# Threshold attention and its expert layer in half batches: order of query tiles, sums, values, units, weight loads

## The chip, the core and the metric

One core of one Trainium2 chip runs the whole kernel. The metric is device time in microseconds from the first to the last instruction with what lies around them; three runs of the kernel before gave a median of 540.56 us (539.83 to 540.8). The engines are TensorE (PE; its weight loads are shown as PEld), VectorE (DVE), ScalarE (ACT), GpSimd (POOL) and SyncE (SP, which here only issues DMAs).

## The reference

```python
batch, n_heads, seq, head_dim = (8, 8, 576, 64)          # q, k, v
scores = scale * np.matmul(q, k.transpose(0, 1, 3, 2))
thresh = np.max(scores, axis=-1, keepdims=True) - tau
scores = np.where(scores >= thresh, scores, -1000000000.0)
scores = scores - np.max(scores, axis=-1, keepdims=True)
attn = np.exp(scores)
attn = attn / (np.sum(attn, axis=-1, keepdims=True) + 1e-09)
attn_out = np.matmul(attn, v)
x = attn_out.transpose(0, 2, 1, 3).reshape(B * S, H * D)  # 4608 x 512
h = x @ w_in                                              # 512 x 2048
g = np.maximum(0.01 * h, h)
out = g @ w_out                                           # 2048 x 512
```

Attention in which only scores within tau = 0.02 of a row's largest count, for 8 batches of 8 heads, and then a two-layer net ("the expert layer") over all 4608 tokens.

## The kernel before

Two heads make a pair, 32 pairs in all, four to a batch. Two pairs make a group c, so that a batch has two groups. A group's 2 x 576 queries are cut into nine query tiles of 128: t = 0 to 3 of the first pair, 4 to 7 of the second, and t = 8, which holds the last 64 queries of both. One such tile is a step; there are 16 x 9 = 144 steps, and nine more turns of the loop in which only what is left over is done. The order of all work is written out by hand in the main loop: engines run their queues in that order.

A step's own work. `s_mm` (L158) makes the scores of the tile, for both heads, in twelve pairs of half-height matmuls over hi and lo parts of q and k (24 small ones where t = 8), into PSUM tiles "s", one of two banks for each head. `s_max` (L181) reduces them on DVE, once per head: sn is the negated scaled score, nmx its least. POOL adds tau (L186, nth). Then either ACT takes the exponent (L191, e), and a step later `s_mask` (L214) masks it on DVE and sums it into den; or, where `direct` is set, ACT alone does both for the second head (L197 far, L201 W). At the end of `s_mask` a transposing DMA on SP's queue (L220) puts the tile's weights W into wT, from which `values` reads.

Work that is spread over the steps:

- `prep` transposes q (i = 0) or k and the two tails (i = 1) of a pair on PE (L129), into the PSUM pair of banks "A", of which there is one; ACT makes hi (L138), DVE makes lo at the end of the step (L139).
- The sums of a group: `sums_0` at t = 0 of the next group on POOL (L228), `sums_1` at t = 1 (reciprocal on DVE, L234, and its fp16 part on POOL, L235), `sums_2` after the step's second reduction (the remainder on DVE, L240), `sums_3` (a matmul that turns the columns into a row, L246, and ACT's copy, L249), and `sums_4` at t = 2 and 4, which spreads the row over partitions (L263, ACT L268, rc). All these use "A".
- `values` at t = 3 and 5 (L279), 20 matmuls each for one pair's 576 queries into "A"; DVE multiplies by rc at the end of that step (L289, xT), and POOL copies the last 64 tokens to xE (L293).
- The expert layer is a list of units. An h unit (`h_unit`, L301, L305) is four matmuls of 512 columns over the four pairs and a leaky rectifier on ACT into gM; sixteen make gM for 512 tokens of a batch. An out unit (`out_mm`, L316) is four of the sixteen matmuls of one output tile of 128 tokens; the fourth part is copied by ACT (L327) and every second tile stored by SP. Tails of two batches share four h units of 16 matmuls with 128 columns, and four out units. Units use the PSUM tiles "u", two banks.

`push_main` puts a batch's 32 units on the list at t = 6 of the group after the batch (the first at step 24), when all four pairs of the batch have their values. `share` weighs how many units each step takes; a step does half of them after its first reduction and half after the second.

Loads: q and k of pair 2c+3 and 2c+4 are issued by SP, one DMA a step (`load_qk`, L81, L86); v by POOL, at steps 1 to 5 for the first batch and at t = 4 to 8 of every even group after that (`load_v`, L96); the 16 pieces of w_in and 16 of w_out by POOL, one each at steps 1 to 32 (`load_w`, L105, L109).

Of the kernel before, what the change touches and what calls it, by code (L numbers as in the profile page):

```python
# [16 lines left out]
def kernel(  # L17
# [17 lines left out]
    NT = 9  # L35
# [14 lines left out]
    sel = sb.tile([128, 18, 64], FP16, name="sel")  # L50
    w_in16 = sb.tile([128, 4, d_ff], FP16, name="win16")
    w_out16 = sb.tile([128, NJ, d_model], FP16, name="wout16")
    gM = sb.tile([128, NJ, 512], FP16, name="gM")
# [7 lines left out]
    nat, qk, wTs, xTs = {}, {}, {}, {}  # L61
# [60 lines left out]
    def prep(p, i, tag="A", bufs=1):  # L122
# [13 lines left out]
        hi = sb.tile([128, N], FP16, tag=f"hi{i}", bufs=3, name=f"hi{i}")  # L136
        lo = sb.tile([128, N], FP16, tag=f"lo{i}", bufs=3, name=f"lo{i}")
# [7 lines left out]
    def s_mm(c, t):  # L145
# [3 lines left out]
        if t < 8:  # L149
            srcs = [(2 * c + t // 4, 0, ds(t % 4 * 128, 128), ds(0, 128))]  # L150
        else:
            srcs = [(2 * c + e, 1, ds(576, 64), ds(64 * e, 64)) for e in range(2)]
# [10 lines left out]
        sc[(c, t)] = out  # L163
# [3 lines left out]
    def s_max(c, t, h, direct):  # L167


        s_ = sc[(c, t)][h]  # L170
        if t == 0 and h == 0:
            dens[c] = sb.tile([128, 18], FP32, tag="den", bufs=2, name="den")
        if h == 0:
            sn = sb.tile([128, 2, 576], FP32, tag="sn", bufs=3, name="sn")
            nmx = sb.tile([128, 2], FP32, tag="nmx", bufs=4, name="nmx")
            nth = sb.tile([128, 2], FP32, tag="nth", bufs=4, name="nth")
            e = sb.tile([128, 2, 576], FP16, tag="e", bufs=3, name="e")
            live[(c, t)] = (sn, nmx, nth, e, Ws[wn[0] % len(Ws)], set())
            wn[0] += 1
        sn, nmx, nth, e, w, masked = live[(c, t)]  # L180
# [13 lines left out]
        else:  # L194
# [8 lines left out]
                accum_out=dens[c][:, 2 * t + h:2 * t + h + 1],  # L203
            )

    def s_mask(c, t):
        sn, nmx, nth, e, w, masked = live.pop((c, t))
        sc.pop((c, t))
        if t == 0:

            wTs[c] = sb.tile([128, 9, 1152], FP16, tag="wT", bufs=2, name="wT")
        for h in range(2):
            if h not in masked:
# [3 lines left out]
                    accum_out=dens[c][:, 2 * t + h:2 * t + h + 1],  # L217
                )
        q0 = 512 if t == 8 else t * 128 + (t // 4) * 128
        nc.sync.dma_start_transpose(out=wTs[c][:, :, ds(q0, 128)], in_=w[:, :])  # L220
# [3 lines left out]
    def sums_0(c):  # L224

        d1 = sb.tile([128, 18], FP32, tag="d1", bufs=1, name="d1")
        rr = sb.tile([128, 18], FP32, tag="rr", bufs=1, name="rr")
        nc.gpsimd.tensor_scalar(out=d1[:, :], in0=dens.pop(c)[:, :], scalar1=1.0, scalar2=1e-9,  # L228
                                op0=OP.mult, op1=OP.add)
        inv[c] = (d1, rr)  # L230

    def sums_1(c):
        d1, rr = inv[c]
        nc.vector.reciprocal(out=rr[:, :], in_=d1[:, :])  # L234
        nc.gpsimd.tensor_scalar(out=r2[:, 0, 0:18], in0=rr[:, :], scalar1=1.0 / RS, scalar2=0.0,  # L235
                                op0=OP.mult, op1=OP.add)

    def sums_2(c):
        d1, rr = inv[c]
        nc.vector.scalar_tensor_tensor(out=r2[:, 1, 0:18], in0=rr[:, :], scalar=1.0 / RS, in1=r2[:, 0, 0:18],  # L240
                                       op0=OP.mult, op1=OP.subtract)

    def sums_3(c):

        t = pair_of_banks().rearrange("p a b -> p (a b)")
# [4 lines left out]
        rows[c] = row  # L250

    def sums_4(c, e):

        row = rows[c]
        t = pair_of_banks().rearrange("p a b -> p (a b)")

        if e == 0:
            parts = [(2 * s, s * 128, 0, 128) for s in range(4)] + [(16, 512, 0, 64)]
        else:
            parts = [(16, 0, 64, 64)] + [(8 + 2 * s, 64 + s * 128, 0, 128) for s in range(3)]  # L260
            parts += [(14, 448, 0, 64), (14, 512, 64, 64)]
# [5 lines left out]
        rc = sb.tile([128, 576], FP32, tag="rc", bufs=2, name="rc")  # L267
        nc.scalar.activation(out=rc[:, :], in_=t[:, 0:576], func=AF.Copy, bias=0.0, scale=1.0)  # L268
        rcs[e] = rc

    def values(c, e):

        b, g = divmod(2 * c + e, NG)
        wT, vb = wTs[c], Vs[b % 2]
        t = pair_of_banks()
        for half in range(2):
            for kb in range(5):
                for h in range(2):
                    nc.tensor.matmul(  # L279
                        out=t[ds(h * 64, 64), half, 0:288], lhsT=vb[:, g, h, kb, :],  # L280
                        rhs=wT[:, 4 * h + kb, ds(e * 576 + half * 288, 288)],
                        start=(kb == 0), stop=(kb == 4), skip_group_check=True,
                    )
        rc = rcs.pop(e)
        x = sb.tile([128, 576], FP16, tag=f"xT{g}", bufs=2, name=f"xT{g}")
        xTs[(b, g)] = x

        def mul():
            nc.vector.tensor_tensor(  # L289
                out=x.rearrange("p (a b) -> p a b", a=2), in0=t[:, :, 0:288],  # L290
                in1=rc.rearrange("p (a b) -> p a b", a=2), op=OP.mult,
            )
            nc.gpsimd.tensor_copy(out=xE[g][:, b, :], in_=x[:, 0:64] if e else x[:, 512:576])  # L293
# [41 lines left out]
    def push_main(b):  # L335

        xs = [xTs[(b, g)][:, ds(g % 2 * 64, 512)] for g in range(NG)]
# [179 lines left out]
```

## Time and profile before

| | us |
|---|---|
| median of three runs | 540.56 |
| span of the profiled execution | 538.3 |
| PE busy | 497.8 (92%) |
| DVE busy | 421.7 (78%) |
| ACT busy | 433.8 (81%) |
| POOL busy | 188.1 (35%) |
| first reduction of step 0 starts | 10.13 |
| first reduction of step 24 starts | 83.03 |
| first reduction of step 126 starts | 426.53 |
| scores of step 143 start | 482.19 |

The span runs from the first to the last instruction of the one profiled execution. Busy time of PE counts the pipelined length of a matmul (380 ns for 512 columns that follow each other every 216 ns or so), so a busy PE need not be at its peak; spacing is read from the starts. In tables of windows, each engine has its busy time and its count of instructions, then come the granted TensorE clock (1.00 is full speed), the mean busy share of the 16 DMA engines and GB/s. In lists of waits, the three numbers are total us, times, and the longest; a weight load (PEld) and the matmul behind it wait for the same thing.

### The profile page before, as it was taken

How to read it: one execution, taken by the hardware profiler on the slowest of the kernel's cores; microseconds unless marked ns; L12 is line 12 of the kernel's file. 1: busy time of each engine (PE TensorE's matmuls, PEld its weight loads, DVE VectorE, ACT ScalarE, POOL GpSimd, SP SyncE). 2: the span in 40 equal slices, each digit the busy share in tenths (PEclk: the TensorE clock that was granted, in tenths of full speed). 3: DMA queues.
4: the chain of work that ended last, by engine and by line, in shares of the span. 5: the costliest groups of instructions: out<-in, count | busy, mean ns of one | idle time of the engine just before them, and what ended most of it. 6: DMA issues, size and time to landing. Idle time of an engine off the chain costs nothing.

```text
span 538.3 us, 12333 instructions
## 1 busy us (share of the span) xinstructions
PE 497.8 (92%) x4384; PEld 272.8 (51%) x4384; DVE 421.7 (78%) x1106; ACT 433.8 (81%) x765; POOL 188.1 (35%) x430
## 2 busy tenths in 40 slices
PE   5678679899999999999999999999999999999996
PEld 3345454454545565454545566455545566445444
DVE  4897989988899878987899878987899878982000
ACT  3887879899878989889888989889888989884622
POOL 0754556443433334222432234323432234331000
PEclk9676969999999999999999999999999999999999
DMA  6999999998998699778999799777998699654001
GB/s 151 150 202 161 175 182 214 200 180 173 172 165 136 139 169 196 140 137 153 183 155 143 132 182 185 142 135 159 183 155 136 132 187 135 111 89 106 39 40 58
DMA packets 266814, 80.50 MB, mean 150 GB/s; under 512 B 251905, under 2 KB 264193, under 8 KB 266753
## 3 DMA queue, kind: packets, MB, share of 16 engines
q1 hardware_dynamic: 249136, 70.68, 72.3%
q0 software_dynamic: 17536, 8.92, 14.2%
q8 instruction: 34, 0.56, 0.4%
q14 instruction: 28, 0.22, 0.1%
q10 hardware_dynamic: 80, 0.13, 0.1%
HBM read 36.70 MB, written 9.44 MB: 86 GB/s over the span
## 4 chain that ended last, share of the span: by engine, by line
PE 43%; ACT 25%; DVE 16%; issue 8%; DMA 4%; POOL 3%; SPq 0%; DVEq 0%; ACTq 0%; POOLq 0%
PE u L316 13%; DVE sn L181 11%; PE u L301 10%; PE s L158 10%; PE A L279 8%; ACT e L191 7%; ACT far L197 5%; ACT W L201 5%; DVE W L214 3%; ACT gM L305 3%; ACT hi L138 3%; POOL nth L186 3%; DMA nat<-in_q_dram 2%; DVE lo L139 1%; ACT rc L268 1%
## 5 line engine op out<-in xcount | busy, mean ns | idle before, releaser
L181 DVE TENSOR_SCALAR_CACHE_REDUCE sn<-s 128x576 f32<-128x576 f32 x288 | 206.5, 750 | 49.3 <-PE s L158 49.1
L186 POOL TENSOR_SCALAR nth<-nmx 128x1 f32<-128x1 f32 x288 | 127.4, 442 | 251.7 <-DVE sn L181 229.5
L191 ACT ACTIVATE e<-sn,nmx 128x576 f16<-128x576 f32 x196 | 150.5, 769 | 32.4 <-DVE sn L181 32.2
L214 DVE SCALAR_TENSOR_TENSOR W<-sn,nth,e 128x576 f16<-128x576 f32 x196 | 155.6, 814 | 0.0
L301 PE MATMUL u<-xT,win 128*128 128x512 f16 x512 | 128.9, 380 | 2.5 <-ACT gM L305 2.5
L316 PE MATMUL u<-wout,gM 128*128 128x512 f16 x512 | 126.2, 380 | 0.0
L158 PEld LDWEIGHTS <-hi 64*128 64x128 f16 (+1 forms) x1280 | 65.1, 99 | 70.2 <-issue 54.9
L158 PE MATMUL s<-hi,hi 64*128 64x288 f16 x512 | 86.2, 300 | 10.3 <-DVE sn L181 8.8
L158 PE MATMUL s<-lo,hi 64*128 64x288 f16 (+1 forms) x640 | 92.2, 294 | 0.0
L158 PE MATMUL s<-hi,lo 64*128 64x288 f16 (+1 forms) x640 | 92.1, 294 | 0.0
L301 PEld LDWEIGHTS <-win 128*128 128x128 f16 x768 | 58.7, 98 | 56.5 <-issue 20.1
L305 ACT ACTIVATE gM<-u 128x512 f16<-128x512 f32 x128 | 74.6, 588 | 11.7 <-PE u L301 11.7
L197 ACT ACTIVATE far<-sn,nth 128x576 f32<-128x576 f32 x92 | 71.0, 771 | 13.8 <-POOL nth L186 11.6
L201 ACT ACTIVATE W<-far,ntau 128x576 f16<-128x576 f32 x92 | 71.3, 775 | 3.0
L316 PEld LDWEIGHTS <-gM 128*128 128x128 f16 x512 | 44.7, 98 | 51.3 <-issue 12.3
L139 DVE SCALAR_TENSOR_TENSOR lo<-A,hi 128x512 f16<-128x512 f32 (+1 forms) x63 | 47.6, 756 | 14.2 <-ACT hi L138 13.7
L129 PE MATMUL A<-I,nat 128*128 128x128 f32 x283 | 44.6, 288 | 9.9 <-DVE lo L139 4.7
L279 PE MATMUL A<-wT,V 128*64 128x288 f16 x640 | 47.5, 297 | 1.5 <-ACT rc L268 1.1
L129 PEld LDWEIGHTS A<-I,nat 128*128 128x128 f32 x283 | 35.2, 147 | 25.2 <-DVE lo L139 10.0
L138 ACT ACTIVATE hi<-A 128x512 f16<-128x512 f32 (+1 forms) x63 | 40.0, 636 | 7.6 <-PE A L129 7.6
L279 PEld LDWEIGHTS <-V 128*64 128x64 f16 x640 | 36.6, 113 | 11.9 <-issue 8.4
L158 PEld LDWEIGHTS <-lo 64*128 64x128 f16 (+1 forms) x640 | 32.1, 99 | 12.6 <-issue 8.9
(44 smaller groups left out, 292.1 us busy)
## 6 DMA issues: line engine op xcount, KB each, us to landing
nat<-in_q_dram SPq DMA_DIRECT2D x32, 256.0 KB, 3.8
nat<-in_k_dram SPq DMA_DIRECT2D x32, 256.0 KB, 3.9
out_dram<-osb SPq DMA_DIRECT2D x16, 512.0 KB, 3.0
wT<-W SPq DMA_TRANSPOSE x144, 3.9
V<-in_v_dram POOLq DMA_DIRECT2D x8, 256.0 KB, 6.1
win<-in_moe_w_in_dram POOLq DMA_DIRECT2D x16, 128.0 KB, 5.2
V<-in_v_dram POOLq DMA_DIRECT2D x16, 128.0 KB, 4.7
wout<-in_moe_w_out_dram POOLq DMA_DIRECT2D x16, 128.0 KB, 4.3
```

The source lines that it names most:

```text
L129: nc.tensor.matmul(out=pt[0:128, ds(c * 128, 128)], lhsT=t[0:128, 4 * i + c, :, :].rearrange("p h d -> p (h d)"), rhs=I32[:, :], is_transp ...
L158: nc.tensor.matmul(out=out[h][po, half, 0:288], lhsT=qk[p][i][a][r, cols], rhs=qk[p][1][b][r, ds(half * 288, 288)], start=(ti == 0), stop= ...
L181: nc.vector.tensor_scalar(out=sn[:, h, :].rearrange("p (a b) -> p a b", a=2), in0=s_[:, :, 0:288], scalar1=-BS, scalar2=None, op0=OP.mult, ...
L186: nc.gpsimd.tensor_scalar(out=nth[:, h:h + 1], in0=nmx[:, h:h + 1], scalar1=1.0, scalar2=tau_f, op0=OP.mult, op1=OP.add,)
L191: nc.scalar.activation(out=e[:, h, :], in_=sn[:, h, :], func=AF.Exp, bias=nmx[:, h:h + 1], scale=-1.0,)
L197: nc.scalar.activation(out=far[:, :], in_=sn[:, h, :], func=AF.Prelu, bias=nth[:, h:h + 1], scale=-1.0, alpha=BIG,)
L201: nc.scalar.activation(out=w[:, ds(h * 576, 576)], in_=far[:, :], func=AF.Exp, bias=ntau[:, 0:1], scale=1.0, accum_out=dens[c][:, 2 * t + ...
L214: nc.vector.scalar_tensor_tensor(out=w[:, ds(h * 576, 576)], in0=sn[:, h, :], scalar=nth[:, h:h + 1], in1=e[:, h, :], op0=OP.is_le, op1=OP ...
L279: nc.tensor.matmul(out=t[ds(h * 64, 64), half, 0:288], lhsT=vb[:, g, h, kb, :], rhs=wT[:, 4 * h + kb, ds(e * 576 + half * 288, 288)], star ...
L301: nc.tensor.matmul(out=t[:, ts(j, N)], lhsT=w_in16[:, gi, ts(j0 + j, 128)], rhs=xs[gi], start=(gi == 0), stop=(gi == NG - 1), skip_group_c ...
L305: nc.scalar.activation(out=g_out, in_=t[:, 0:nj * N].rearrange("p (j n) -> p j n", j=nj), func=AF.Prelu, bias=0.0, scale=1.0, alpha=0.01)
L316: nc.tensor.matmul(out=t[:, :], lhsT=g_in(j), rhs=w_out16[:, j, :], start=(j == 0), stop=(j == NJ - 1), skip_group_check=True,)
```

## The change

A batch is worked through in 18 steps instead of two groups of nine. Its steps go through four sets of tiles G = (b, gi): gi = 0 and 1 are the first two query tiles of the pairs 0, 1 and of the pairs 2, 3 (four steps each), gi = 2 and 3 are the tail tile and the other two query tiles of the same pairs (five steps each). So after eight steps the first half of the queries of all four pairs are done.

- Sums, the row and its spreading are done for each G: four chains in a batch, at t = 5, 9, 14 and 1 of the next batch, on 8 or 10 columns. `sums_3` and `sums_4` take their PSUM tile from "u" and no longer from "A".
- `values` runs for each G in two parts of ten matmuls, 256 or 320 columns wide, in two steps that follow each other; one multiplication on DVE ends both.
- The units come by half batch u: eight h units of eight matmuls with 256 columns, and eight out units. `push_main(b, 0)` comes at t = 12 of the batch itself (the first at step 12), `push_main(b, 1)` at t = 6 of the next. gM is two tiles of half the size. The number of units and of their rectifiers is the same.
- Units a step come from a rate that looks at every push to come; `share` and the choice of direct steps are new.
- `prep` runs at steps 0 to 5 for the pairs 1 to 3 of the first batch; hi and lo have four buffers and wT three, for three and two.
- v of the first batch is issued ahead of step 0, later ones at t = 12 to 16; the pieces of w_in at steps 0 to 10 and of w_out at 11 to 18, up to two a step; pair 3 wholly at step 0, the pairs of the next batch at t = 2 to 17.

```diff
+    def place(st):
+        b, i = divmod(st, NS)
+        gi = 0 if i < 4 else 1 if i < 8 else 2 if i < 13 else 3
+        pos = i - (0, 4, 8, 13)[gi]
+        e = pos // 2 if gi < 2 else (pos - 1) // 2
+        tile_c = pos % 2 if gi < 2 else 2 + (pos - 1) % 2
+        tail = gi > 1 and pos == 0
+        return (b, gi), pos, 4 * b + gi % 2 * 2, e, tile_c, tail
...
-    def sums_3(c):
-        t = pair_of_banks().rearrange("p a b -> p (a b)")
+    def sums_3(G):
+        t = bank()
...
-    def sums_4(c, e):
-        row = rows[c]
-        t = pair_of_banks().rearrange("p a b -> p (a b)")
+    def sums_4(G, e):
+        row = rows[G]
+        t = bank()
...
-        for half in range(2):
-            for kb in range(5):
-                for h in range(2):
-                    nc.tensor.matmul(
-                        out=t[ds(h * 64, 64), half, 0:288], lhsT=vb[:, g, h, kb, :],
-                        rhs=wT[:, 4 * h + kb, ds(e * 576 + half * 288, 288)],
+        for kb in range(5):
+            for h in range(2):
+                nc.tensor.matmul(
+                    out=t[ds(h * 64, 64), e, 0:N], lhsT=vb[:, g, h, kb, :],
+                    rhs=wT[:, 4 * h + kb, ds(e * N, N)],
...
-        for j in range(NJ):
-            units.append((1, lambda j=j: h_unit(512, xs, gM[:, j:j + 1, :], j, 1)))
+        for j in range(0, NJ, 2):
+            units.append((1, lambda j=j: h_unit(256, xs, gM[:, j:j + 2, :], j, 2)))
...
+        for i in range(5):
+            load_v(0, i)
+        share = (22, 22, 22, 22, 13, 13, 27, 13, 13, 27, 13, 13, 22, 22, 22, 13, 13, 22)
+        for b in range(B):
+            pushes[NS * b + 12] = 16
+            pushes[NS * b + 24] = 16 + 4 * (b % 2 == 1 or b > 1) + 4 * (b == B - 1)
...
+                    st = 2 * j + i - 2 if b == 0 else o + ((-6, -5), (-4, -1), (0, 1), (2, 3))[j][i]
+                    if st >= 0:
+                        preps[st] = (4 * b + j, i)
...
+                st = o + (4, 8, 13, 18)[gi]
+                close[st] = G
+                chain[st + 1] = G
+                spread[st + 2] = (G, 0)
+                if gi > 1:
+                    spread[st + 3] = (G, 1)
+                v0 = o + (7, 10, 15, 22)[gi]
+                (early if gi < 2 else late)[v0] = (G, 0)
+                early[v0 + 1] = (G, 1)
...
+        for i in range(32):
+            w_at.setdefault(i * 11 // 16 if i < 16 else 11 + (i - 16) // 2, []).append(i)
...
-                    direct = tau_f <= 16.0 and (
-                        t not in (3, 7) if c < 3 else t in (3, 5) or not any(u[0] for u in units[:n]))
+                direct = tau_f <= 16.0 and (
+                    t not in (3, 7) if st < 12 else t in (5, 8, 11, 16) or not any(u[0] for u in units[:n]))
```

In a step the order is now: scores; `prep` (in the first batch); the `early` values; the first reduction; `sums_1`; the first half of the units; `prep`; the `late` values; `sums_4`; the second reduction; `sums_2`, all but one of the second half of the units, `sums_3` and that unit where a chain falls; else the second half of the units; `s_mask` of the step before; lo and the multiplication; `sums_0`; loads.

More of the change, by code (lines that the diff above doesn't have):

```diff
@@ L222, with cols_of @@
     inv, rows, rcs = {}, {}, {}
[L224 to L228, printed above, removed]
[L229 to L235 removed]
+    def cols_of(G):
+        return 8 if G[1] < 2 else 10
@@ new lines @@
+            if st in chain:
+                sums_1(chain[st])
+            work(n - n // 2)
+            if pi is not None:
+                prep(*pi)
+            if st in late:
+                values(*late[st])
+            if st in spread:
+                sums_4(*spread[st])
+            if not last:
+                s_max(st, 1, direct)
+            if st in chain:
+                sums_2(chain[st])
+                work(n // 2 - 1)
+                sums_3(chain[st])
+                work(1 if n > 1 else 0)
+            else:
+                work(n // 2)
```

302 lines of the change are left out of this document (166 added, 136 removed).

## The prediction

> **What bounds the kernel now.** I read the table of windows first, cut at steps: a step is one query tile, 144 in all, and it starts where the first reduction of L181 starts. The cuts are step 0 (10.13), 12, 24, 36 (123.03), 54, 72, 90, 108, 126 (426.53), and 482.19, where the scores of step 143 start.
>
> ```profile
> core 0: us, PE busy (x) PEld busy (x) DVE busy (x) ACT busy (x) POOL busy (x), PEclk, DMA share, GB/s
> 10.13:46.03 35.90, 25.88 (x192) 14.98 (x191) 31.27 (x83) 29.21 (x50) 20.38 (x42) 0.71 1.13 176
> 46.03:83.03 37.00, 27.52 (x276) 17.56 (x276) 33.69 (x89) 28.95 (x50) 18.87 (x41) 0.82 1.14 176
> 83.03:123.03 40.00, 37.65 (x337) 19.90 (x336) 35.74 (x95) 36.35 (x66) 19.94 (x43) 1.00 1.25 194
> 183.20:243.70 60.50, 59.55 (x573) 33.78 (x573) 52.61 (x138) 53.76 (x97) 21.32 (x49) 1.00 0.91 160
> 482.19:538.30 56.11, 51.42 (x341) 26.07 (x340) 6.42 (x17) 22.40 (x39) 2.29 (x7) 0.99 0.20 59
> ```
>
> Three stages. Steps 0 to 23 (72.9 us) have no expert units: DVE leads (31.3 of 35.9), PE's clock is partly halved. From step 24 on units fill PE; a batch of 18 steps takes 60.2 to 61.2 us, mean 60.7 over steps 36 to 125, with PE busy 98%. After step 143, 56 us remain in which PE works nearly alone. Now PE's stream and DVE's, for prices (the second column is the length, so spacing is read from the starts):
>
> ```profile
> 245.02 1.03 PE L316 MATMUL u<-wout,gM 128*128 128x512 f16 x4
> 245.98 0.30 PE L158 MATMUL s<-hi,hi 64*128 64x288 f16 x2
> 246.12 0.28 PE L158 MATMUL s<-hi,lo 64*128 64x288 f16 x2
> ...
> 246.61 0.29 PE L158 MATMUL s<-lo,hi 64*128 64x288 f16 x2
> 246.82 1.90 PE L316 MATMUL u<-wout,gM 128*128 128x512 f16 x8
> 249.33 0.23 PE L246 MATMUL A<-I,r 128*128 128x128 f16 x1 [0.61 <-DVE r L240]
> ```
> ```profile
> 183.98 0.71 PE L129 MATMUL A<-I,nat 128*128 128x128 f32 x5
> 184.52 1.03 PE L316 MATMUL u<-wout,gM 128*128 128x512 f16 x4
> ```
> ```profile
> 317.95 1.06 PE L301 MATMUL u<-xE,win 128*128 128x128 f16 x16
> ```
> ```profile
> 481.15 0.75 DVE L181 TENSOR_SCALAR_CACHE_REDUCE sn<-s 128x576 f32<-128x576 f32 x1
> 481.83 0.81 DVE L214 SCALAR_TENSOR_TENSOR W<-sn,nth,e 128x576 f16<-128x576 f32 x1
> 482.57 0.82 DVE L214 SCALAR_TENSOR_TENSOR W<-sn,nth,e 128x576 f16<-128x576 f32 x1
> 483.31 0.75 DVE L181 TENSOR_SCALAR_CACHE_REDUCE sn<-s 128x576 f32<-128x576 f32 x1
> ```
>
> A 512-wide matmul is spaced (1.03-0.38)/3 = 0.217, so a unit of four is 0.866; a 128-wide one (1.06-0.22)/15 = 0.056; a transpose 0.54/5 = 0.108; a pair of score matmuls 0.122. A change between tiled shapes (64*128 or 128*64) and the full array costs 0.09 more (the last pair of scores is followed after 0.21, not 0.12). DVE: reduction 0.68, mask 0.74; lo 0.61 or 0.74, xT 0.67 in the same way. Waits of PE and its weight loads in the 303.5 us of steps 36 to 125:
>
> ```profile
> PE u L301 <- ACT gM L305: 2.0, 8, 0.3
> PEld L246 <- DVE r L240: 8.9, 10, 1.4
> ```
>
> So the one real wait of steady state is the matmul of the sums, 0.89 us each, two a batch. Check by addition, PE of one batch: 18 scores x (6 x 0.122 + 2 x 0.093) = 16.6; 34 units x 0.866 + 2 tail units of 16 x 0.056 = 31.2; 36 transposes 3.9; 4 values x (10 x 0.122 + 0.095) = 5.2; sums 1.1: 58.0. With waits of 2 x 0.89 = 1.8 and 0.9 of small ones it is the measured 60.7. PE sets the steady state.
>
> **The change, part by part.**
> *Units by half batch.* The same 288 units, 128 of them now 8 matmuls of 256 columns. No row has that width; the bounds are 8 x 0.056 (too little) and 8 x 0.217; interpolating 0.056 at 128 and 0.217 at 512 gives 0.109, a unit 0.87. Cost 0.1 a batch. ACT's Prelu stays 128x512.
> *Values by half.* Eight blocks of ten matmuls for four of twenty, the same columns. The six that run right after the scores add one change of shape (0.095), the two in mid-step two (0.19): 0.95 for 0.38, +0.57 a batch.
> *Sums by half batch.* Four chains a batch for two. One more matmul of 0.06 each is little; the wait is not. From the first score matmul of the step to the sums' matmul I find 2.85 to 3.57 us (three cases; 245.98 to 249.33 is 3.35): scores, reduction, reciprocal, reduction, remainder on DVE. In front of it PE now has: t=5, scores 0.83, half a value block 0.75, one unit: 2.45, DVE on time: wait 0.4. t=9, two units: 2.56, but steps 7 and 8 carry 2.8 and 3.5 us of DVE against 2.54 of PE in every other batch, so DVE comes late: 1.2. t=14 and t=1, one unit and a transpose block: 2.3, waits 0.9 and 1.0. Sum 3.5 a batch against 1.8. Behind the waiting matmul stand units and the next scores, so DVE and ACT wait too. Bounds: 4 x 0 and 4 x 1.4 (the longest seen).
> *Sums in the unit banks.* Ten tiles a batch move from A to u, two buffers. A unit after such a tile reuses the bank of the unit just before it, and waits for its Prelu. Bounds: none, or ten waits of 0.3; about three fall where PE has nothing between: 0.8.
> *Push.* Units of t=12 may need an xT that DVE finishes just then: 0.2.
> Steady batch: 58.0+0.1+0.6+0.1 = 58.8 of PE, +3.5+0.8+0.9+0.2 = 64.2 (bounds of the waits: 61 to 67). Masks and direct rows stay alike (196 to 198 masks).
> *Steps 0 to 23.* Transposes of three pairs of a batch crowd into steps 0 to 5, two sum chains fall before step 12. DVE's sum by step (ACT's where larger) is 33.8 for steps 0 to 11 and 38.7 for 12 to 23, against 32.0 and 33.7 before; measured before were 35.9 and 37.0, 7.2 above the sums, since PE at half clock and the sums lengthen the loop of scores and reductions. With more PE work the half clock shrinks, so I add 3.1 and 1.8: 36.9 and 40.5, +4.5. In return 16 units are done by step 36; steps 24 to 35: 40.5 for 40.0.
> *Loads.* Five V issues (0.68 each on POOL) go ahead of step 0, hidden in POOL's first idle 9.7 us; their bytes share the DMA engines with pairs 1 and 2, which lands them some us later, still ahead of their transposes at steps 0 to 3: 0.4 (0 to 2). Pair 3's four loads go into SP's queue at step 0, ahead of the first transposing DMA, which isn't ready yet. Weights come one or two a step (0.57 each on POOL, which is busy 57% there): nothing waits for POOL but the small nth. No cost taken, up to 6 if DMA chokes.
> *The end.* At step 143's scores before, 53 units were left; after, 3+12+24 = 39: 33.8, with scores 0.83, values 1.6, sums 0.5, one xT 0.3 and the last copy and store 4.6 (533.7 to 538.3): 41.8 for 56.1, -14.3.
>
> Sum against the span of 538.3: +0.4 +4.5 +0.5; steps 36 to 53 (two units fewer) 62.5 for 60.2, +2.3; steps 54 to 125 4 x 64.2 = 256.8 for 243.3, +13.5; steps 126 to 143's scores 58.1 for 55.7, +2.4; end -14.3. Together +9.3: span 547.6. The median of the runs is 2.3 above the profiled span: **549.9**, say 549.5.
>
> Two rules. The rows show the 128-wide matmuls at 0.056 although each has a weight load of 0.098. The Trainium skill (TensorE: Matmul & The Clock Gate, Back-to-back issue gap) gives about 81 ns for a load and matmul pair at N=128 in a real kernel, 25 ns above this row; on the added 1024 narrow matmuls that would be 25.6 us and 575. The windows show a granted clock of 0.71 and 0.82 in steps 0 to 23, so (1-0.71) x 2 x 35.9 + (1-0.82) x 2 x 37.0 = 34 us at half. The same page (Terms) puts the penalty at throttled time x (1 - K/N), 17 us; by it, ending the half clock would give back 17, not the 2.3 of my sum, and 535.
>
> **Rivals.**
> 1. The waits don't grow: the sums' chain is covered as now, PE's loss stays 2.7 a batch. Batch 61.5; changes +0.4, +2.5, 0, -0.4, +2.7, 0, -14.3: 529.2, with 2.3 **531.5**, faster. For it: DVE has 13% idle in steady state, and half batches let lateness average out. Against: the wait is met at all ten chains looked at. It decides below about 0.6 us of added waits a batch (2.7 in my sum). 22%.
> 2. Loads choke: DMA share is 1.1 to 1.25 already, and by step 18 some 3 MB more (14 weights, V, a pair) must pass at about 200 GB/s seen; with transposing DMAs (3.9 us) landing after 6 or more, values before step 12 and first units wait: +8, **557**. Against: landings of 4 to 7 us there show little queueing. 10%.
> 3. In between, gains and waits cancel: waits 2.1 below my sum a batch: **540.5**. 6%.
> 4. Clock: PE is what the half clock holds up; 34 us at half are 17 us of cycles, and all come back: 549.5 + 2.3 - 17 = **535**. Against: DVE is busy 33.7 of 37.0 us there. 3%.
> 5. Weight loads show between narrow matmuls: 512 more at up to 0.098 exposed, half of it taken: 25 us, **575**. Against: the 0.056 row. 2%.
> The forecast has 57%, its own range 542 to 557.
>
> A difference under 0.2% (1.1 us) can't be told from none. Faster: rivals 1 and 4, less their spill into none: 0.23. Same: 0.06. Slower: the rest, 0.71. For eight in ten the range reaches down to rival 1 and up past rival 2: 531 to 559.
>
> **What would show it.** The sums' matmul with four waits a batch of 0.4 to 1.2 each; 18 steps taking 63 to 65 us from step 54 on with PE's idle on that line and on unit banks; 256-wide matmuls spaced 0.109; steps 0 to 23 in 76 to 79 us; 42 us from the last scores to the end. A batch at 61.5, or an added 256-wide spacing over 0.12, makes it wrong.

## The result, and the profile after

| | before | after |
|---|---|---|
| median of the runs taken side by side, us | 540.43 (four) | 581.93 (four: 576.51 to 582.95) |
| ratio, 95% interval | | 1.0755 [1.0708, 1.0802] |
| span of the profiled execution, us | 538.3 | 579.3 |
| PE / DVE / ACT / POOL busy, us | 497.8 / 421.7 / 433.8 / 188.1 | 511.0 / 425.5 / 442.3 / 192.1 |

The change makes the kernel slower by 7.5%, 41.5 us. PE is busy 13.2 us longer; the rest of the 41 us in the span is time in which PE does nothing. Medians here and below are of all runs; the ratios leave out one slow run, the 576.31 us of the kernel with the sums behind all units.

The table of windows of the changed kernel, cut as before at steps 0, 12, 24, 36 and 54, then steps 72 to 89, and last the stretch from the scores of step 143 on (engines' busy time and count, granted clock, DMA share, GB/s):

```profile
12.70:51.89 39.19, 28.37 (x236) 16.43 (x236) 32.36 (x87) 29.61 (x52) 19.32 (x45) 0.78 1.14 175
51.89:102.17 50.28, 39.67 (x344) 23.77 (x343) 36.95 (x99) 34.30 (x63) 22.57 (x53) 0.90 1.11 162
102.17:145.25 43.08, 39.21 (x406) 25.24 (x404) 33.62 (x93) 36.41 (x67) 15.80 (x37) 1.00 1.00 158
145.25:210.20 64.95, 60.72 (x622) 38.13 (x621) 53.63 (x146) 53.50 (x97) 22.11 (x53) 1.00 0.83 150
276.00:342.80 66.80, 62.01 (x638) 39.71 (x636) 53.91 (x146) 54.53 (x99) 22.12 (x53) 1.00 0.81 143
534.94:579.30 44.36, 37.59 (x305) 24.76 (x303) 6.48 (x17) 18.66 (x34) 2.54 (x9) 0.99 0.29 67
```

DVE's work grew by 1 to 3 us in the first two windows and in a batch (32.36 for 31.27, 36.95 for 33.69, 53.91 for 52.66 in steps 72 to 89), these windows by 3 to 13: steps 12 to 23 went from 37.0 to 50.3 us. Put in one table, with the prediction's terms (the last row starts at step 143's scores, the one above ends there):

| stage | before | predicted | after | after - predicted |
|---|---|---|---|---|
| to step 0's first reduction | 10.1 | 10.5 | 12.7 | +2.2 |
| steps 0 to 23 | 72.9 | 77.4 | 89.5 (39.2 and 50.3) | +12.1 |
| steps 24 to 35 | 40.0 | 40.5 | 43.1 | +2.6 |
| steps 36 to 53 | 60.2 | 62.5 | 64.9 | +2.4 |
| steps 54 to 125, four batches | 243.3 | 256.8 | 265.3 (65.8, 66.8, 65.8, 67.0) | +8.5 |
| 126 to the scores of 143 | 55.7 | 58.1 | 59.4 | +1.3 |
| from there to the end | 56.1 | 41.8 | 44.4 | +2.6 |
| span | 538.3 | 547.6 | 579.3 | +31.7 |

So 22 us of the loss against before, and 8.5 of the miss, lie in the four steady batches; 14.3 of the miss lie ahead of step 24.

PE's waits in the steady batches, steps 54 to 125 (total us, times, longest), changed kernel:

```profile
PE u L334 <- ACT gM L338: 5.6, 20, 0.5
PE u L265 <- ACT gM L338: 4.7, 4, 1.3
PE u L265 <- DVE r L259: 2.7, 8, 0.8
PE u L349 <- ACT osb L360: 2.0, 4, 0.5
PE u L349 <- ACT row L268: 1.4, 2, 0.7
PE u L334 <- ACT row L268: 1.4, 2, 0.7
PE u L334 <- ACT gE L338: 0.9, 2, 0.5
```

Before, the same list held 4.5 us in all for those steps:

```profile
PE A L246 <- DVE r L240: 2.5, 6, 0.6
PE u L301 <- ACT gM L305: 1.4, 6, 0.3
PE A L279 <- ACT rc L268: 0.6, 4, 0.2
```

Now it holds 18.7: 2.7 for the remainder, and 16.0 for something that ACT has yet to copy out of a bank of "u": a unit's rectifier (gM, gE), an output (osb) or the row. (A list counts from the modelled end of the matmul ahead, so a wait measured from start to start is 0.1 to 0.2 longer.) L265 is the matmul of the sums, L334 an h unit, L349 an out unit. Two things are to be seen. The sums' matmul itself waits for a rectifier, once a batch, at t = 9, for 1.0 or 1.3 us, because the bank it is given still holds a unit. And units wait for the row, or for the unit just before them.

The timeline of step 78 of the changed kernel shows both (start, length, engine, line, operation, then in brackets the idle time before and its releaser; rows of weight loads, DVE, POOL and SP are left out, and so are rows of PE and ACT where dots stand):

```profile
296.39 0.23 PE L265 MATMUL u<-I,r 128*128 128x128 f16 x1
296.46 1.03 PE L349 MATMUL u<-wout,gM 128*128 128x512 f16 x4
297.15 0.78 ACT L209 ACTIVATE far<-sn,nth 128x576 f32<-128x576 f32 x1 [0.42 <-POOL nth L198]
...
297.95 0.78 ACT L213 ACTIVATE W<-far,ntau 128x576 f16<-128x576 f32 x1
...
298.73 0.26 ACT L268 ACTIVATE row<-u 128x128 f16<-128x128 f32 x1
298.89 0.59 ACT L360 ACTIVATE osb<-u 128x512 f32<-128x512 f32 x1
299.04 1.91 PE L334 MATMUL u<-x,win 128*128 128x256 f16 x16 [0.71 <-ACT row L268]
...
300.78 0.39 PE L282 MATMUL u<-row,sel 128*128 128x128 f16 x4
300.98 0.60 ACT L338 ACTIVATE gM<-u 128x512 f16<-128x512 f32 x1 [0.28 <-PE u L334]
...
301.63 1.03 PE L334 MATMUL u<-x,win 128*128 128x256 f16 x8 [0.46 <-ACT gM L338]
```

The sums' matmul ran at 296.39. Its tile is 128 columns, and the next matmul follows after 0.07 us, but it holds a whole bank until ACT has copied the row, and on ACT's queue far and W come first: the copy starts 2.3 us later, at 298.73. The next unit but one needs that bank and stands still for 0.71 us. At 300.78 the spreading of the row (L282) takes a bank too, and the unit behind it waits 0.46 us for the rectifier of the unit ahead of it, which began only at 300.98.

### The profile page after: what moved, and what is told of

Read it like the earlier page. It is cut to its first block, busy times and chain, and to the rows that moved or that the text cites. A ratio compares the mean times of both kernels' runs of the same rounds, so it can differ in the third digit from the quotient of the medians.

```text
span 579.3 us, 13405 instructions
## 1 busy us (share of the span) xinstructions
PE 511.0 (88%) x4896; PEld 316.7 (55%) x4896; DVE 425.5 (73%) x1142; ACT 442.3 (76%) x793; POOL 192.1 (33%) x462
## 3 DMA queue, kind: packets, MB, share of 16 engines
q1 hardware_dynamic: 249136, 70.68, 68.5%
## 4 chain that ended last, share of the span: by engine, by line
PE 46%; ACT 20%; DVE 18%; issue 6%; DMA 6%; POOL 2%; SPq 0%; DVEq 0%; ACTq 0%
PE u L349 16%; PE s L169 13%; PE u L334 11%; DVE sn L193 10%; ACT e L203 6%; DVE W L227 5%; ACT gM L338 4%; PE A L309 4%; ACT W L213 3%; ACT far L209 3%; DMA nat<-in_q_dram 2%; DMA wT<-W 2%; PE A L129 2%; POOL nth L198 2%; DMA wout<-in_moe_w_out_dram 1%
## 5 line engine op out<-in xcount | busy, mean ns | idle before, releaser
L334 PE MATMUL u<-x,win 128*128 128x256 f16 x1024 | 131.2, 274 | 12.9 <-ACT gM L338 9.5
L334 PEld LDWEIGHTS <-win 128*128 128x128 f16 x1280 | 110.1, 98 | 51.0 <-issue 40.3
L349 PE MATMUL u<-wout,gM 128*128 128x512 f16 x512 | 130.2, 383 | 7.2 <-DMA wout<-in_moe_w_out_dram 3.9
L169 PEld LDWEIGHTS <-hi 64*128 64x128 f16 (+1 forms) x1280 | 62.9, 98 | 57.0 <-issue 44.1
L169 PE MATMUL s<-lo,hi 64*128 64x288 f16 (+1 forms) x640 | 89.1, 291 | 2.0 <-DVE lo L139 2.0
L169 PE MATMUL s<-hi,lo 64*128 64x288 f16 (+1 forms) x640 | 89.0, 290 | 0.0
L169 PE MATMUL s<-hi,hi 64*128 64x288 f16 x512 | 83.0, 296 | 5.7 <-ACT hi L138 3.1
L338 ACT ACTIVATE gM<-u 128x512 f16<-128x512 f32 x128 | 74.1, 589 | 12.8 <-PE u L334 12.1
L349 PEld LDWEIGHTS <-gM 128*128 128x128 f16 x512 | 44.2, 98 | 57.8 <-issue 22.8
L309 PE MATMUL A<-wT,V 128*64 128x320 f16 (+1 forms) x640 | 52.6, 295 | 3.3 <-DMA wT<-W 3.3
L309 PEld LDWEIGHTS <-V 128*64 128x64 f16 x640 | 31.0, 111 | 23.1 <-issue 16.4
L322 DVE TENSOR_TENSOR x<-A,rc 128x512 f16<-128x512 f32 (+1 forms) x32 | 24.1, 753 | 16.5 <-PE A L309 11.1
```

Source lines behind the costliest of these rows:

```text
L169: nc.tensor.matmul(out=out[h][po, half, 0:288], lhsT=qk[p][i][a][r, cols], rhs=qk[p][1][b][r, ds(half * 288, 288)], start=(ti == 0), stop= ...
L309: nc.tensor.matmul(out=t[ds(h * 64, 64), e, 0:N], lhsT=vb[:, g, h, kb, :], rhs=wT[:, 4 * h + kb, ds(e * N, N)], start=(kb == 0), stop=(kb ...
L334: nc.tensor.matmul(out=t[:, ts(j, N)], lhsT=w_in16[:, gi, ts(j0 + j, 128)], rhs=xs[gi], start=(gi == 0), stop=(gi == NG - 1), skip_group_c ...
L338: nc.scalar.activation(out=g_out, in_=t[:, 0:nj * N].rearrange("p (j n) -> p j n", j=nj), func=AF.Prelu, bias=0.0, scale=1.0, alpha=0.01)
L349: nc.tensor.matmul(out=t[:, :], lhsT=g_in(j), rhs=w_out16[:, j, :], start=(j == 0), stop=(j == NJ - 1), skip_group_check=True,)
```

## The experiments

All ratios are against the kernel before, run side by side. Unless it says otherwise, an edit is made in the changed kernel. The first four kernels separate the suspects: the sums' tiles, the wait for DVE's remainder, the loads.

**The sums left out.**

```diff
+    rcK = sb.tile([128, 2, 320], FP32, name="rcK")
...
-            rc = rcs.pop(G)
+            rc = rcK
...
-            if st in spread:
-                sums_4(*spread[st])
...
-                sums_3(chain[st])
```

> Leaves out the sums' matmul, the row and its spreading (the values are multiplied by a constant instead); reciprocals and remainders stay on DVE and POOL. Theory B (the ten tiles a batch that moved into the two unit banks make units wait for ACT) and theory R (the sums' matmul waits for the remainder on DVE) both say that the steady batch falls from 66 us to 59 to 60.5, and the time to 533 to 543. Rival D (PE is late because DVE and ACT are unevenly loaded by the new order, whatever the sums do): batch at 64 or more, time 565 or more.

Measured 545.72, 1.0113 [1.0064, 1.0162]: 36.2 us less than the changed kernel, and just above the 533 to 543 expected. Two of the four batches of steps 54 to 125 take 60.0 us for 65.8; the other two (63.5 and 62.4 for 66.8 and 67.0) lose 3.1 us to values that wait for a transposing DMA of wT. Of the 5.8 us of an undisturbed batch 1.1 is PE's own work on the sums (the price in the prediction, for two chains; four take little more), and some 4.7 are waits. But this also takes out the wait for DVE, and ACT's copies, so it can't say which of the three it is.

**The remainder not waited for.** The same matmul of the sums reads a constant tile.

```diff
-        nc.tensor.matmul(out=t[:, 0:128], lhsT=r2[:, :, :].rearrange("p a b -> p (a b)"),
+        nc.tensor.matmul(out=t[:, 0:128], lhsT=r2K[:, :, :].rearrange("p a b -> p (a b)"),
```

> The sums' matmul reads a constant tile in place of the remainders (so sums come out wrong); it no longer waits for DVE, but row and spreading use the unit banks as before. Theory R as the main cause: batch 66 to 61, time 545. Theory B as the main cause: the batch falls by 2 to 3 us only, to 63.5 to 64.5, time 560 to 568.

Measured 583.34, 1.0795 [1.0747, 1.0843]: nothing gained, less than either expectation. Two of its four batches of steps 54 to 125 are 0.8 us shorter, and one is 1.4 longer, in which values wait 1.5 for wT. PE's longest waits in this kernel, from 151 to 481 us:

```profile
PE u L335 <- ACT gM L339: 7.4, 22, 0.6
PE u L266 <- ACT gM L339: 6.0, 5, 1.3
PE u L335 <- ACT gE L339: 2.6, 3, 0.9
PE u L350 <- ACT osb L361: 2.0, 4, 0.5
```

The remainder is gone from the list. The matmul of the sums (here L266) waits for its bank at t = 9 as long as in the changed kernel (6.0 us in five waits, from 145 to 470 us there), so that wait doesn't hang on the remainder. The remainder had taken 3.7 us there; the waits of h units for gM and gE grew from 7.4 us to 10.0 and took up most of that. The wait that the prediction put at 3.5 us a batch is not what costs the time here.

**V later.** v of the first batch at steps 1 to 5, as before, and v of the second at steps 19 to 23.

```diff
-        for i in range(5):
-            load_v(0, i)
...
+            if 0 < st < 6:
+                load_v(0, st - 1)
+            if 18 < st < 24:
+                load_v(1, st - 19)
```

> Only loads are moved: v of the first batch to steps 1 to 5 (as before), v of the second to steps 19 to 23. Theory L (early loads crowd the DMA engines, first pair and w_out come late): first reduction at 10.1 to 10.5 us for 12.7, stalls of steps 16 and 20 smaller, time 570 to 575. If the crowd is made by weights and pairs alone, only the start comes back: 578 to 580. Batch of steady state unchanged at 66.

Measured 580.0, 1.0724 [1.0684, 1.0763]. The start is back at 10.1 us, so the V ahead of step 0 is what costs 2.6 there; but the first values then wait for V, 1.5 us in step 7; steps 0 to 11 take 42.6 for 39.2, and step 36 begins at 144.3 us for 145.2. The time moves, it isn't won.

**The sums behind all units of their step.**

```diff
-            if st in spread:
+            if st in spread and t == 16:
                 sums_4(*spread[st])
...
-                work(n // 2 - 1)
+                work(n // 2)
                 sums_3(chain[st])
-                work(1 if n > 1 else 0)
...
+            if st in spread and t != 16:
+                sums_4(*spread[st])
```

> Sums' matmul and spreading stand behind all units of their step, ahead of the next scores (the spreading of t=16 excepted). Theory B and R: the scores of 0.9 us now lie between a sums tile and the next unit, and the remainder has a unit more of time, so the batch falls from 66 to 61.5 to 63, time 548 to 560. Rival D: waits move in front of the scores and DVE gets its scores later; batch 65 to 67, time 575 or more.

Measured 571.31, 1.0535 [1.0475, 1.0596]. The batches take 63.6 to 65.0 us, 1.9 to 2.2 less, where I had hoped for more. Scores and reductions now lie between a sums' tile and the next unit, which covers part of ACT's copies. The wait of L265 for a rectifier is down to 0.3 us, once, from 145 to 470 us, but units still wait 8.2 us for gM (6.0 in the changed kernel): out of one pool of two, every sums' tile still leaves one bank for the stream of units.

The next four ask whether it is the banks themselves, and what the loads share in it.

**The tiles left out, ACT's copies kept.** As the first kernel, but row and rc are copied from a constant tile.

```diff
+    rcF = sb.tile([128, 512], FP32, name="rcF")
...
-        t = bank()
-        nc.tensor.matmul(out=t[:, 0:128], lhsT=r2[:, :, :].rearrange("p a b -> p (a b)"),
-                         rhs=I16[:, :], start=True, stop=True, skip_group_check=True)
+        t = rcF
```

> As a1, but ACT still makes its copies of row and spread sums, from a constant tile in SBUF; only the matmuls of the sums and their ten bank tiles a batch are left out. Theory B (units wait for a bank): batch stays at 60 to 62.5 as in a1, time 543 to 550. Rival A (the added copies on ACT make it late): batch 65 to 66.5, time 570 or more.

Measured 556.26, 1.0297 [1.0246, 1.0347] (two runs), above the 543 to 550 expected. The undisturbed batches take 60.5 for 60.0 without the copies: the copies' time on ACT is 0.5 us a batch. The total is higher than that mostly because steps 12 to 23 took 53.2 us here, for 47.4 without the copies, which is the matter of the loads below. One profile is a poor measure of these steps: in six kernels whose loads are those of the change (the changed one, this one, the first two here, the one with the sums behind all units, and the last one below) they take from 43.5 to 53.8 us, step 16 from 4.5 to 11.3 and step 20 from 5.3 to 10.4.

**The kernel before, with the sums' tiles in "u".** The positive control: nothing of the change but this. The row takes one bank, each spreading two (576 columns don't fit one), ten tiles a batch, as many as in the changed kernel.

```diff
-        t = pair_of_banks().rearrange("p a b -> p (a b)")
+        t = bank()
...
+        for lo_, hi_ in ((0, 512), (512, 576)):
+            t = bank()
+            for i, q0, r0, n in parts:
+                if lo_ <= q0 < hi_:
...
+            nc.scalar.activation(out=rc[:, lo_:hi_], in_=t[:, 0:hi_ - lo_], func=AF.Copy, bias=0.0, scale=1.0)
```

> The kernel before, with its sums' tiles in the unit banks (one for the row, two for each spreading, as 576 columns need 512 and 64): ten tiles a batch in u as in the changed kernel, order and loads as before. Theory B: the batch grows from 60.7 to 63 to 65, time 557 to 572. Rival (the new order makes the waits, not the banks): batch 60.5 to 61.5, time 539 to 545.

Measured 587.86, 1.0883 [1.0863, 1.0902]: 48 us slower than the kernel before (539.88 beside it), from this alone, and more than expected. Its batches of 18 steps take 67.8 us for 60.5 to 61.2, and the first 24 steps 72.8 for 72.9: where there are no units to share the banks with, nothing is lost. PE's waits there, from 126.4 to 464.7 us (L266 is the spreading, L246 the matmul of the sums):

```profile
PE u L266 <- ACT gM L307: 11.8, 10, 1.4
PE u L266 <- ACT rc L270: 8.8, 8, 1.4
PE u L246 <- ACT gM L307: 4.0, 5, 0.8
PE u L303 <- ACT rc L270: 3.6, 12, 0.3
```

All four are waits for a bank. The two parts of a spreading stand closer together than in the changed kernel, so these 7 us a batch are not a price to be carried over, but they show that the move by itself can cost as much as the whole loss of the steady batches.

**Twelve pieces of w_out left out.** The out units read the four that are loaded.

```diff
-                out=t[:, :], lhsT=g_in(j), rhs=w_out16[:, j, :],
+                out=t[:, :], lhsT=g_in(j), rhs=w_out16[:, j % 4, :],
...
-                load_w(i)
+                if i < 20:
+                    load_w(i)
```

> Only the first 4 of 16 pieces of w_out are loaded and used for all (12 loads of 128 KB left out; the output is not the reference's). Theory L: the stall of step 20 (9.9 us) falls to 3.5 and that of step 16 (7.4) to 3.5 to 5, steps 12 to 24 take 40 to 43 instead of 50.3, time 570 to 574. If the stalls are not from the weight loads, steps 12 to 24 stay at 47 or more.

Measured 576.83, 1.0677 [1.0645, 1.071] (two runs), less gained than expected; the interval just touches that of the changed kernel. Step 20 takes 4.0 us for 9.9, less than in any kernel with all pieces loaded as in the change, but step 16 stays at 7.55, and the start is later, 14.4: of the 6 us won there 3.6 are left in the span. What stops the changed kernel in those two steps is seen in its timeline of PE:

```profile
68.83 0.98 PE L309 MATMUL A<-wT,V 128*64 128x320 f16 x10 [3.30 <-DMA wT<-W]
...
84.27 0.80 PE L349 MATMUL u<-wout,gM 128*128 128x512 f16 x2 [0.35 <-DMA wout<-in_moe_w_out_dram]
88.60 1.21 PE L349 MATMUL u<-wout,gM 128*128 128x512 f16 x2 [3.52 <-DMA wout<-in_moe_w_out_dram]
```

and in some of what POOL and SP issue around it:

```profile
66.08 1.09 POOL L109 DMA_DIRECT2D wout<-in_moe_w_out_dram  x2
67.07 6.28 SPq L233 DMA_TRANSPOSE wT<-W  x1
74.52 1.09 POOL L109 DMA_DIRECT2D wout<-in_moe_w_out_dram  x2
76.20 1.12 POOL L109 DMA_DIRECT2D wout<-in_moe_w_out_dram  x2
80.05 1.12 POOL L109 DMA_DIRECT2D wout<-in_moe_w_out_dram  x2
```

Read together, the rows make a chain. In step 16 values wait 3.3 us for weights W that are still on their way: their transposing DMA was issued at 58.33 and landed at 68.79. The whole loop stops, and with it POOL's next loads, which are issued at 74.52 (those before, at 61.94 and 66.08, were 4.1 us apart). The last two pieces of w_out go out from 80.05 on and land at 88.6 and 89.2, where the second out tile has been waiting for them. The issue of one transposing DMA held SP's queue for 6.28 us, with 202 GB/s moving from 66.5 to 75 us.

**Sums at the end, V and weights spread out.** The kernel with the sums behind the units, with V late, and two weight pieces a step at steps 0 to 15.

```diff
-            w_at.setdefault(i * 11 // 16 if i < 16 else 11 + (i - 16) // 2, []).append(i)
+            w_at.setdefault(i // 2, []).append(i)
```

> a6 with v of the first batch at steps 1 to 5, v of the second at steps 19 to 23, and all weights at two a step from step 0 to 15. Theory L with B: first reduction at 10.1 to 10.5, steps 12 to 24 in 40 to 43, batch 63.5 to 65 as in a6, time 554 to 562. If DMA is short whatever the order: 565 to 572.

Measured 567.97, 1.0529 [1.0494, 1.0564]: the same as the sums at the end alone, whose ratio is 1.0535, and not the 554 to 562 hoped for. Steps 12 to 23 came down to 39.2, steps 0 to 11 went up to 46.9 and 24 to 35 to 45.1; step 36 begins at 141.2 us for 140.8. With all bytes to be moved, another order of the loads moved the wait to other steps (3.0 us for V in step 7, 2.9 for wT in step 11) and took nothing off. Step 33, the longest of steps 24 to 35 at 7.2 us, is no matter of loads: a unit waits 1.9 us there for the bank of an output, and as long in the kernel with the sums at the end alone.

The last four ask for the sizes, and for a version that beats both.

**Few loads.** V late, and four of the 16 pieces of either weight: 24 loads left out.

```diff
-                load_w(i)
+                if i < 4 or 16 <= i < 20:
+                    load_w(i)
```

> The changed kernel with v of the first batch at steps 1 to 5, v of the second at steps 19 to 23, and 4 of 16 pieces each of w_in and w_out loaded and used for all (24 loads left out, output not the reference's). Theory L, upper bound of what short DMA costs: first reduction at 10.1, step 36 at 131 to 136 instead of 145, later batches at 65.8 and 66.8 as before, time 564 to 570. If little of the early loss is DMA: step 36 at 140 or later, 573 or more.

Measured 572.28, 1.0588 [1.0564, 1.0613]: 9.7 us less than the changed kernel, just above the 564 to 570 expected. Steps 12 to 23 take 40.1 us, step 36 begins at 134.7 for 145.2. The batches are unchanged to 0.1 us. So about 10 us are the share of the loads, V ahead of step 0 among them. How long the transposing DMAs of wT took from issue to landing up to 110 us (least, median, most), before, changed, and with few loads:

```profile
DMA to landing us min/median/max: 3.3/5.2/9.0
```
```profile
DMA to landing us min/median/max: 3.2/6.0/13.0
```
```profile
DMA to landing us min/median/max: 3.2/4.4/8.7
```

**Few loads and no sums.** The first kernel and the last one together.

> a1 (no sums' matmuls, no bank tiles for them) with the few loads of a12. If banks and DMA are the two causes and add: first step 36 at 129 to 134, batch 60 to 62.5, time 528 to 537, so faster than the kernel before. If a third cause of this size is left: 543 or more.

Measured 538.35, 0.9965 [0.9952, 0.9978], 43.6 us less than the changed kernel; singly the two took 36.2 and 9.7, 45.9. The two causes are nearly additive. It isn't a version to use (sums and weights are missing), and it leaves out work that the kernel before does: 1.1 us of sums on PE in each of eight batches, about 9 us. Without these the two causes account for some 35 of the 41.5 us. What remains against the kernel before, by stages: +8.4 us up to step 36, +3.7 over steps 36 to 142, -13.9 from step 143 on.

**The kernel before, its sums' matmul behind all units of the step.** A wait that is plainly in the profile, 0.9 us twice a batch by the list of weight loads, is given cover.

```diff
                     sums_2(c - 1)
-                    work(n // 2 - 1)
+                    work(n // 2)
                     sums_3(c - 1)
-                    work(1 if n > 1 else 0)
```

> The kernel before with one edit: the sums' matmul stands behind all units of its step instead of ahead of the last one. Before, PE waited for the remainder 16 times, 0.9 us each. If that wait is PE's own loss, a unit of 0.87 now covers it: batch 60.7 to 59.0 to 59.8, time 527 to 534. Rival: PE then reaches the next scores before DVE is done, and the wait moves there: time 538 to 541.

Measured 538.92 (eight runs), 0.9965 [0.9952, 0.9979]: it beats both kernels with the whole computation done, by 0.35%, and by far less than expected. The batches take 60.1, 60.5, 60.4, 60.5 and 61.1 us, the same as before but for the third, which took 61.2. PE's waits in it, from 183 to 427 us:

```profile
PE u L301 <- ACT gM L305: 3.9, 6, 0.8
PE A L279 <- ACT rc L268: 0.6, 4, 0.2
PE A L263 <- ACT row L249: 0.4, 1, 0.4
```

The wait for the remainder, 2.5 us in that stretch before, is gone; the wait for a rectifier grew from 1.4 to 3.9, all of it in the steps of the edit (t = 1). A unit less between the sums and the step's end is a unit more in a row before them, and ACT is late for that one. The rival's time came, but not its mechanism: no wait of the scores for DVE is in the list. And the wait was worth less than 0.9 us from the start: read from the starts of matmuls, as spacings were, the ten of steps 36 to 125 cost PE 0.56 us each.

**Three banks for "u".** The changed kernel whole, with "A" one bank and "u" three. Values multiply each part by itself, their second part stands behind the first half of the units, and the fifth transpose of k goes to "u" with a copy of its own.

```diff
-        return ps.tile([128, 512], FP32, tag="u", bufs=2, name="u")
+        return ps.tile([128, 512], FP32, tag="u", bufs=3, name="u")
...
-        if e == 0:
-            vals[G] = pair_of_banks()
-        t = vals[G]
+        t = ps.tile([128, 512], FP32, tag="A", bufs=1, name="A")
...
-                early[v0 + 1] = (G, 1)
+                late[v0 + 1] = (G, 1)
```

> The changed kernel whole, with a third bank for the units: A is one bank instead of two (each part of the values has its own tile and multiplication and stands behind the first half of the units; the tail's transpose of a k block goes to u with its own copies on ACT and DVE). Sums stay in u where the change put them, loads as in the change. Theory B (two banks for ten sums tiles and the units a batch are too few): the batches of 65.8 and 66.8 fall to 61 to 63.5, time 545 to 562, in spite of four more copies each on ACT and DVE and A's single bank. Rival (order and sums as such, not the number of banks): 65 or more, 575 or more.

Measured 557.75, 1.0329 [1.0296, 1.0361]: 24.2 us less than the changed kernel, although it adds copies and multiplications. Its batches take 62.7 to 64.7 us, 2.1 to 3.0 less; steps 12 to 23 take 43.5 for 50.3. PE's waits from 200 to 450 us (L272 the sums' matmul, L337 and L352 units):

```profile
PE u L272 <- DVE r L266: 3.9, 10, 0.7
PE u L337 <- ACT gM L341: 3.8, 10, 1.0
PE u L352 <- ACT osb L363: 2.0, 4, 0.5
```

The sums' matmul has its bank in time and is back to waiting for the remainder, 0.4 us a time. With a third bank about half of the loss of a batch is taken back. The values' multiplications and second parts come at other times too, and their share was not tried apart. What steps 12 to 23 gained can't be put down to the bank: it lies within what these steps differ by from kernel to kernel.

## Why the prediction was right or wrong

Slower was right, and it was the side that the forecast took, but in the steady batches for another reason than it gave, so the side owes something to luck. The size was not right: 581.93 lies 23 us above the top of the range, 31.7 above the forecast in the span. Point by point.

*The units of 256 columns: right.* Sixteen matmuls of L334 in a row (at 299.04 above) take 1.91 us, and a single one 0.27: (1.91-0.27)/15 = 0.109 us, the value interpolated. With them rival 5 falls: no weight load shows. This too is where a figure of the Trainium skill (TensorE: Matmul & The Clock Gate, Back-to-back issue gap) can be held against rows: its 81 ns at N=128 for pairs in a real kernel isn't met by the 0.056 us of the prediction's row at 317.95, while the formula it gives for isolated matmuls, N/2.4 + 2.5 ns, which is 109 at 256, is what this row shows with a weight load for each. (The prediction's 1024 "added" narrow matmuls are all that there are; 512 were added, as its rival 5 says.)

*PE's own work in a batch, 58.0 + 0.8: right.* Summed by the spacings, it comes to 58.8 to 59.0 in the changed kernel as well.

*"Sums by half batch", 3.5, and "Sums in the unit banks", 0.8: this is the step that failed in the steady batches.* Batches average 66.3 us: 7.5 above the work, where the prediction had 5.4 of waits. The more telling part is which. The list of waits gives 16.0 us in four batches to banks and 2.7 to the remainder: 4.0 and 0.7 a batch, the reverse of 0.8 and 3.5. The 0.89 a time that stood for the kernel before was itself misread: it is from the list of weight loads (PEld), whose idle time begins at the end of the load before, while matmuls still run (PE's own bracket at 249.33 is 0.61). Read from the starts it is 0.56. In the changed kernel, read in the same way, the matmul's waits for the remainder at t = 5, 14 and 1 are 0.1, 0.4 or 0.9, and 0.3 us, for 0.4, 0.9 and 1.0 forecast. At t = 9, where DVE was to come 1.2 us late, the matmul does wait about that long, but for a rectifier, with the remainder made a constant as well; that the size agrees is luck.

The runs say the same. With the remainder's wait taken away the batch is no shorter on average; with the sums' tiles and their work taken away an undisturbed one is 5.8 shorter, and only 0.5 of that comes back with ACT's copies; the tiles alone, put into "u" in the kernel before, cost 7.0. The prediction saw that "a unit after such a tile reuses the bank of the unit just before it", and counted ten rectifiers of 0.3, three of them felt. It left out two things that the timeline shows. A small tile holds its bank not for its own 0.06 us but until ACT has copied it, and ACT's copy stands behind far and W, 1.6 us of them. And the sums' matmul waits for a bank too, up to 1.3 us, before it can begin; the upper bound of 10 x 0.3 was no bound. (By the terms given, the bounds of a batch were 59.9 to 68.5 and not 61 to 67.)

*"Loads. No cost taken, up to 6 if DMA chokes": failed, and with it "Steps 0 to 23", +4.5.* Steps 0 to 23 took 16.6 us more than before. Values in step 16 wait for wT, out units in step 20 for w_out; with 24 loads left out and V later step 36 begins 10.6 us earlier, and steps 0 to 23 take 80.3 for 89.5, which is 9.2 of the 12.1 missed there. This is what rival 2 described, at 10% and +8; it came on top of the other loss and not in its place. The prediction read landings of 4 to 7 us as "little queueing", but the transposing DMAs of the kernel before had a longest of 9.0, at a DMA share of 1.13 to 1.25 and 176 to 194 GB/s, and it priced 3 MB more as if they had room.

*V ahead of step 0, 0.4 (0 to 2): mis-sized.* It was 2.6, and up to 4.3 in the other kernels that have V there: with V at steps 1 to 5 the first reduction starts at 10.1 again. The first block of k of pair 0 landed at 8.15 us for 5.68. The prediction asked only about pairs 1 and 2, while the bytes that step 0 itself waits for were on the same DMA engines. V is wanted soon all the same: put later, the first values waited for it.

*Steps 0 to 11, 1 us more expected, 3.3 measured.* PE's waits in this stretch of the changed kernel:

```profile
PE u L265 <- DVE r L259: 3.6, 2, 2.8
PE s L169 <- ACT hi L138: 2.3, 2, 1.3
PE s L169 <- DVE lo L139: 2.0, 3, 0.9
```

The sums' row is the longest, but without the sums these steps take 40.3 us for 39.2, so it isn't what costs. The prediction added up engines' work by step. But q and k are now transposed one step ahead of their use, so that scores wait for hi and lo (steps 1 and 3 take 4.1 us for 2.9); work that is just in time has an order, which a sum doesn't see.

*The end, 41.8: nearly right.* 44.4 (the terms given add up to 41.6). Of the 14.3 us foreseen 11.7 came. They are real, and would have been the gain of the change.

*The clock.* From the windows, (1-0.78) x 2 x 39.2 + (1-0.90) x 2 x 50.3 = 27 us are at half, 34 before; the time of these steps went up all the same. The plainest case is the kernel with few loads: its steps 12 to 23 run at a granted clock of 1.00 for 0.82 before, and take 40.1 us for 37.0. So rival 4 falls: PE's clock was not what held them. By the penalty that the Trainium skill gives (TensorE: Matmul & The Clock Gate, Terms), 7 us less at half would be worth an estimated 3.5; no run here shows that gain.

*Rivals 1 and 3* needed waits that don't grow, or grow little; the batch, at 65.8 to 67.0 and not at 61.5, answers both.

What stays open: the 8.4 us by which even the kernel with few loads and no sums is behind before step 36. Its list up to there has 2.9 and 2.5 us of waits of the scores for hi and lo, 5.7 for reductions, and 2.3 of values for V (step 25), but no run takes them apart.

## What to carry to other kernels

A tile's price in a rotating pool is the time from its allocation to the end of its reader, with all that stands ahead of that reader in its queue; a tile of 0.06 us in a pool of two stops the main stream, here, whenever that time is longer than one tile's work, so count pools by holding time before moving anything into them. Waits of the busiest engine don't add up as gains or losses: the one removed is followed by the next that was hidden under it, and only a run that takes one away (a constant in its place) tells its worth. When loads are drawn forward, first look for the longest landing in the stretch they move to, and for what the program's very first step waits for.

## What the runs showed that was not expected

Transposing DMAs land late in company: from issue to landing 3.6 us in the median once loads are rare (at most 6.5, from 145 to 500 us in the changed kernel), up to 13.0 us among the weight loads, while plain loads of w_out took 4.1 to 8.5. And the issue itself of one such DMA can hold SP's queue, 1.25 to 6.28 us, so that the loads of q and k behind it go out later as well.

Two waits in every batch, 0.9 us each by one list and 0.56 by the starts, and 0.35% of the time: that is what covering the plainest wait of the kernel before was worth.

The rule that groups of matmuls should rotate through different PSUM banks so that one's copying overlaps the next one's work (the Trainium skill, Perfetto Trace Analysis, Matmuls) agrees with the 2.1 to 3.0 us a batch that came back with three banks; what the runs add is that a small tile that ACT copies late can take one of two banks out of the rotation for 2.6 us, from its matmul at 296.39 to the next unit in its bank at 299.04.
